# Regrouping the token chunks of a retention-plus-MLP kernel: the first chunk of every sequence first, decay in the mask, weights loaded by turns, a trailing output layer in group 0

## The chip, the cores and the metric

One core of a Trainium2 chip runs the whole program. The metric is the device time in microseconds (us). A profile gives in addition the span from the first to the last instruction of one execution, some 2 us less than its device time. "Granted clock" is the share of TensorE's full clock that the profile records. Engines are named as in the profile: PE is TensorE (matmuls), PEld its weight loads, ACT is ScalarE, DVE is VectorE, POOL is GpSimd. `L217` is line 217 of the kernel that the profile belongs to.

## The reference

```python
# q, k, v: (4 sequences, 8 heads, 768 positions, 64), float32
for t in range(S):                                   # a decaying state, one step per position
    state = gamma * state + k[t] outer v[t]          # gamma per head, 1 - 2**(-5-h)
    y[t]  = q[t] @ state / sqrt(64)
x = y as (3072 tokens, 512)
h = x @ w_in                                         # 512 x 2048
g = h + sin(alpha * h)**2 / (alpha + 1e-9)
out = g @ w_out                                      # 2048 x 512
```

## The kernel before

A sequence is cut into six chunks of 128 positions, 24 chunks in all. Inside a chunk the recurrence becomes two matrix products with a triangular mask. A state carries it from chunk to chunk, so chunk c needs the chunks before it in its sequence. For each chunk the stages are T (transposes of q and k), A (scores times mask, into `aT`) and M (scores times V, the state's part, the update of the state, the scaled result into `xT`).

Finished chunks form groups. For a group of up to four chunks (512 columns) the first layer runs as 16 tiles f = 0..15. Meanwhile the attention of the next group and the output layer of the previous one run in the gaps.

```python
groups = [3, 2, 4, 4, 4, 4, 3]                       # chunks of each group, in the sequences' order

def ff_in(g, f, square):                             # one first-layer tile
    ph = psum.tile([128, n], F32, name="ph", tag="mm", bufs=4)
    for i in range(KS):                              # KS = 4
        nc.tensor.matmul(ph, w_in[...f...], xT[g][:, i, :], ...)          # L217
    nc.scalar.activation(out=s, in_=ph, func=ACTF.Sin, ...)               # L220
    # square of s on ACT (L222) or on DVE (L224)
    return lambda: nc.vector.scalar_tensor_tensor(gT[g][:, f, :], s, rec_alpha[...], ph, ...)   # L225

def ff_out(g, ts, f):                                # one of 16 output steps of one chunk
    if f == 0:
        po[g, ts] = psum.tile([128, d_model], F32, name="po", tag="mm", bufs=4)
    nc.tensor.matmul(po[g, ts], gT[g][:, f, ...], w_out[:, f, :], start=(f == 0), stop=(f == FF - 1))   # L234
```

In PSUM the kernel gives the scores `pa` 128x1024 float32, the attention output `ty` 128x512, the state `ps` 128x256, and the rotating tag `mm` four buffers of 128x512. A bank in this document is one such buffer of 512 float32 columns; `pa` is as large as two. First-layer tiles (`ph`) and output accumulators (`po`) share the four of `mm`. A `ph` bank is free only after the `gT` update, three engine steps later; a `po` bank only after 16 steps.

V is multiplied by a decay (`kg`) before use. GpSimd does this for chunks 9 to 23, and VectorE for the early ones. Loads are issued by GpSimd, in this order: chunks 1 and 2, three quarters of w_in, chunk 3, the last quarter, chunk 4, four quarters of w_out, the other chunks.

Of the kernel before, what the change touches and what calls it, by code (L numbers as in the profile page):

```python
# [15 lines left out]
def kernel(  # L16
# [12 lines left out]

    nc = tc.nc  # L30
# [9 lines left out]
    assert S % C == 0 and D == 64 and H % 2 == 0 and d_model == 512  # L40
    scale = 1.0 / math.sqrt(D)
# [3 lines left out]
    groups = [3, 2, 4, 4, 4, 4, 3]  # L45
    assert sum(groups) == NJ
    NG = len(groups)
    first = [sum(groups[:g]) for g in range(NG)]
    group_of = [g for g, n in enumerate(groups) for _ in range(n)]
# [19 lines left out]
    def load(name, src, j):  # L69
        t = big.tile([128, H, D], BF16, name=f"{name}r", tag=f"{name}r", bufs=NJ)  # L70
        nc.gpsimd.dma_start(out=t, in_=chunk_of(src, j))  # L71
        raw[name, j] = t

    def load_chunk(j):
        for name, src in (("q", q), ("k", k), ("v", v)):
            load(name, src, j)
# [13 lines left out]
    for name, src in (("q", q), ("k", k)):  # L90
        near[name] = big.tile([128, H, D], F32, name=f"{name}0")
        nc.sync.dma_start(out=near[name], in_=chunk_of(src, 0))
        raw[name, 0] = big.tile([128, H, D], BF16, name=f"{name}b")
# [7 lines left out]
    load("v", v, 0)  # L101
# [5 lines left out]
    nc.vector.tensor_scalar(ident, tio, pos[:, 0:1], None, op0=ALU.is_equal)  # L107

# [5 lines left out]
    lg = consts.tile([128, H], F32, name="lg")  # L114
    for h in range(H):
        nc.vector.memset(lg[:, h:h + 1], lng[h])
# [4 lines left out]
    for p in range(NP):  # L121
        nc.scalar.activation(out=qg[:, 0, p, :], in_=tio, func=ACTF.Exp, scale=lgp[:, p:p + 1])
    kg = consts.tile([128, NCH, H], F32, name="kg")
    nc.scalar.activation(out=kg, in_=expo, func=ACTF.Exp, scale=-1.0)
    step = consts.tile([128, NCH, NP], F32, name="step")
    for c in range(1, NCH):
        nc.scalar.activation(out=step[:, c, :], in_=lgp, func=ACTF.Exp, scale=float(C * c))
# [4 lines left out]
    mask01 = consts.tile([128, 128], BF16, name="mask01")  # L132
    nc.vector.tensor_scalar(mask01, tio, pos[:, 0:1], None, op0=ALU.is_ge)
    mask_bc = mask01[:, None, :].to_broadcast([128, H, 128])
# [10 lines left out]
    def scale_v(j, eng):  # L145
        eng.tensor_mul(raw["v", j], raw["v", j], kg[:, j % NCH, :, None].to_broadcast([128, H, D]))  # L146

    def open_T(j, tag="ty", bufs=1):
        st["pt", j] = psum.tile([128, 2 * NP, 128], BF16, name="pt", tag=tag, bufs=bufs)
        st["qkT", j] = work.tile([128, 2 * NP, 128], BF16, name="qkT", tag="qkT", bufs=3)  # L150

    def half_T(j, i):
        for p in range(NP):
            nc.tensor.transpose(st["pt", j][:, i * NP + p, :],  # L154
                                raw["qk"[i], j][:, 2 * p:2 * p + 2, :].rearrange("p h d -> p (h d)"), ident)

    def stage_T(j):
        open_T(j)
        half_T(j, 0)
        half_T(j, 1)  # L160
        nc.scalar.copy(st["qkT", j], st["pt", j])  # L161

    def stage_A(j):
# [8 lines left out]
        nc.vector.tensor_mul(aT.rearrange("p e n t -> p (e n) t"), pa.rearrange("p e n t -> p (e n) t"), mask_bc)  # L172
        st["aT", j] = aT

    def stage_M(j):
        b, c = divmod(j, NCH)
        g = group_of[j]
        if j == first[g]:
            xT[g] = work.tile([128, KS, groups[g] * C], BF16, name="xT", tag="xT", bufs=3)
# [12 lines left out]
        last = c == NCH - 1  # L192
        if not last:
            if c == 0:
                st["ps"] = psum.tile([128, NP, D], F32, name="ps", tag="ps")
            ps = st["ps"]
            for p in range(NP):
                for e in range(2):
                    nc.tensor.matmul(ps[64 * e:64 * e + 64, p, :], raw["k", j][:, 2 * p + e, :], vs[:, 2 * p + e, :],  # L199
                                     start=(c == 0 and p == 0), stop=True, skip_group_check=True)  # L200
        o = (j - first[g]) * C
        nc.vector.tensor_mul(xT[g][:, :, o:o + C], py, qg[:, c])  # L202
        if not last:
            for e in range(2):
                r = slice(64 * e, 64 * e + 64)
                nc.scalar.copy(s_bd[(c + 1) % 2][r, :, r], ps[r, :, :])  # L206
# [4 lines left out]
    def ff_in(g, f, square):  # L211
        n = groups[g] * C
        if f == 0:
            gT[g] = work.tile([128, FF, n], BF16, name="gT", tag="gT", bufs=2)
        ph = psum.tile([128, n], F32, name="ph", tag="mm", bufs=4)
        for i in range(KS):
            nc.tensor.matmul(ph, w_in[:, i, f * 128:(f + 1) * 128], xT[g][:, i, :],  # L217
                             start=(i == 0), stop=(i == KS - 1))
        s = work.tile([128, n], F32, name="s", tag="s", bufs=4)
        nc.scalar.activation(out=s, in_=ph, func=ACTF.Sin, scale=alpha_sb[:, f:f + 1])  # L220
        if square == "A":
            nc.scalar.activation(out=s, in_=s, func=ACTF.Square)  # L222
        else:
            (nc.vector if square == "D" else nc.gpsimd).tensor_mul(s, s, s)  # L224
        return lambda: nc.vector.scalar_tensor_tensor(  # L225
            gT[g][:, f, :], s, rec_alpha[:, f:f + 1], ph, op0=ALU.mult, op1=ALU.add)

    out_view = out.rearrange("(t p) n -> p t n", p=128)
    po = {}

    def ff_out(g, ts, f):
# [4 lines left out]
        if f == FF - 1:  # L236
            o_sb = work.tile([128, d_model], F32, name="o_sb", tag="o_sb", bufs=3)
            if g == NG - 1 and ts == groups[g] - 1:
# [5 lines left out]
            nc.sync.dma_start(out=out_view[:, first[g] + ts, :], in_=o_sb)  # L244

    def out_pieces(g):
        if g == 0:
            todo = [(ts, f) for f in range(FF) for ts in (0, 1)] + [(2, f) for f in range(FF)]
        else:
            todo = [(ts, f) for ts in range(groups[g]) for f in range(FF)]  # L250
        return [lambda ts=ts, f=f: ff_out(g, ts, f) for ts, f in todo]


    LATE = 9
    todo = [lambda j=j: load_chunk(j) for j in (1, 2)]
    todo += [lambda i=i: load_w_in(i) for i in range(3)]
    todo += [lambda: load_chunk(3), lambda: load_w_in(3), lambda: load_chunk(4)]
    todo += [lambda i=i: load_w_out(i) for i in range(WP)]
    todo += [lambda j=j: load_chunk(j) for j in range(5, LATE)]
    for j in range(LATE, NJ):  # L260
        todo += [lambda j=j: load_chunk(j)]
        if j > LATE + 1:
            todo += [lambda j=j: scale_v(j - 2, nc.gpsimd)]
    todo += [lambda j=j: scale_v(j, nc.gpsimd) for j in (NJ - 2, NJ - 1)]
    for fn in todo:
        fn()
# [5 lines left out]
    def idle_work(n, w=512):  # L272
        for _ in range(n):
            nc.tensor.matmul(scratch[:, :w], warm[:, :128], warm[:, :w], start=True, stop=True)  # L274


    idle_work(9)
    nc.vector.tensor_copy(raw["q", 0], near["q"])
    open_T(0, "mm", 4)
    half_T(0, 0)  # L280
    nc.scalar.copy(st["qkT", 0][:, :NP, :], st["pt", 0][:, :NP, :])
    nc.vector.tensor_scalar_mul(qg[:, 0], qg[:, 0], scale)
    decay_table(1)
    idle_work(6)
    nc.vector.tensor_copy(raw["k", 0], near["k"])
    half_T(0, 1)
    nc.scalar.copy(st["qkT", 0][:, NP:, :], st["pt", 0][:, NP:, :])
    scale_v(0, nc.vector)
    idle_work(4)
    stage_A(0)  # L290
    open_T(1, "mm", 4)
    half_T(1, 0)
    half_T(1, 1)
    nc.scalar.copy(st["qkT", 1], st["pt", 1])
    scale_v(1, nc.vector)
    for t in s_bd:
        nc.vector.memset(t, 0.0)
    idle_work(3)
    stage_M(0)
    idle_work(1)  # L300
    stage_A(1)
    open_T(2, "mm", 4)
    half_T(2, 0)
    idle_work(2)
    half_T(2, 1)
    nc.scalar.copy(st["qkT", 2], st["pt", 2])
    scale_v(2, nc.vector)
    nc.tensor.transpose(pal, alpha_row, ident_f)
    idle_work(3)
    stage_M(1)  # L310
    idle_work(1)
    stage_A(2)
    nc.scalar.copy(alpha_sb, pal)
    sin0 = consts.tile([128, 1], F32, name="sin0")
    nc.scalar.activation(out=sin0, in_=warm[:, 0:1], func=ACTF.Sin)
    decay_table(2)
    nc.vector.tensor_scalar_add(rec_alpha, alpha_sb, 1e-9)
    nc.vector.reciprocal(rec_alpha, rec_alpha)
    idle_work(5)
    stage_M(2)  # L320
    idle_work(3)


    def phase(g, outs, att, squares):

        no, done = len(outs), 0
        for f in range(FF):
# [4 lines left out]
            while done < no * (f + 1) // FF:  # L332
                outs[done]()
                done += 1

# [14 lines left out]

    phase(0, [], {2: [G(3)], 5: [G(4)], 9: [T(3), V(3)], 11: [A(3)], 13: [G(5)]}, "AAD")
    outs = out_pieces(0)
    stage_T(4)
    scale_v(4, nc.vector)
    for fn in outs[:4]:
        fn()
    stage_A(4)
    stage_M(3)
    for fn in outs[4:8]:
        fn()  # L360
    stage_M(4)
    phase(1, outs[8:], {7: [T(5), V(5)], 8: [A(5)], 9: [T(6), V(6)], 10: [A(6), M(5)], 11: [T(7), V(7)],
                        12: [A(7), M(6)], 13: [T(8), V(8)], 14: [A(8), M(7)]}, "AAAD")
    stage_M(8)
    for g in range(2, NG):
        att = {}
        if g + 1 < NG:
            js = list(range(first[g + 1], first[g + 1] + groups[g + 1]))
# [40 lines left out]
```

## Time and profile before

| | before |
|---|---|
| device time, median of 3 runs | 235.52 us (234.64 to 238.43) |
| profiled span, mean granted clock | 233.0 us, 0.997 |
| PE busy | 214.8 us, 92% of the span |
| PE's largest wait: first-layer matmul for a gT update | 3.5 us in 5 waits |

The page of the kernel before, its table of 40 time slices (5.8 us each; a digit is the busy share in tenths; PEclk is the granted clock in tenths):

```profile
PE   7998867988889998999999999999999999999992
PEclk9999999999999999999999999999999999999998
```

PE has gaps in the first 16 slices (to about 93 us) and is full afterwards. A change can therefore gain only in the first 93 us, or by taking PE work away.

The same by stage, from the windows view of the kernel before. Columns: stretch, its length, then busy time and count of PE, PEld, DVE, ACT and POOL, granted clock, DMA share, GB/s. The borders are the first Sin of groups 0, 1, 2 and 3:

```profile
0.00:18.40 18.40, 16.43 (x154) 8.67 (x157) 12.91 (x39) 10.27 (x25) 14.65 (x23) 1.00 1.46 159
18.40:39.90 21.50, 16.26 (x152) 9.47 (x151) 17.77 (x30) 16.97 (x34) 10.74 (x14) 1.00 1.69 187
39.90:65.60 25.70, 22.97 (x247) 14.75 (x251) 18.13 (x32) 19.92 (x41) 23.28 (x26) 1.00 2.34 150
65.60:94.40 28.80, 26.75 (x240) 13.96 (x242) 22.34 (x29) 23.92 (x39) 28.80 (x33) 1.00 1.75 125
94.40:233.00 138.60, 132.39 (x955) 66.93 (x969) 75.62 (x104) 96.83 (x160) 6.90 (x7) 1.00 0.18 44
```

Groups 0 and 1 leave PE idle for 5.2 and 2.7 us. The last row is the dense part.

PE's waits in the kernel before (line, what it waited for: us in total, times, longest):

```profile
PE ph L217 <- DVE gT L225: 3.5, 5, 1.3
PE ph L217 <- DVE xT L202: 2.3, 4, 0.8
PE pa L169 <- ACT qkT L161: 2.0, 6, 0.6
```

The timeline of the kernel before at the start of group 1, with two output accumulators open, which leaves two `mm` banks for first-layer tiles (start, duration, engine, line, operation; in brackets, how long the engine was idle before and what released it):

```profile
40.12 0.60 PE L217 MATMUL ph<-xT,w_in 128*128 128x256 bf16 x4
...
40.76 0.47 ACT L220 ACTIVATE s<-ph,alpha_sb 128x256 f32<-128x256 f32 x1
...
41.27 0.42 ACT L222 ACTIVATE s<-s 128x256 f32<-128x256 f32 x1
...
41.72 0.48 DVE L225 SCALAR_TENSOR_TENSOR gT<-s,rec_alpha,ph 128x256 bf16<-128x256 f32 x1 [0.39 <-ACT s L222]
...
42.25 0.60 PE L217 MATMUL ph<-xT,w_in 128*128 128x256 bf16 x4
```

This is one life of a bank: matmuls at 40.12, Sin, square, gT update, and the same bank's next tile at 42.25 us. That is 2.13 us per bank for 256 columns, or one tile in about 1.07 us with two banks.

### The profile page before, as it was taken

The page shows a single profiled execution, that of the slowest core. Times are in us where ns is not written, and L with a number is a line of the kernel's source. Part 1 is how long each engine was busy: PE and PEld are TensorE (multiplying, and loading weights), DVE is VectorE, ACT ScalarE, POOL GpSimd, SP SyncE. Part 2 cuts the span into 40 slices and gives each one's busy share as a digit, 9 for nine tenths or more (in the row PEclk, how much of TensorE's full clock was granted, in tenths as well). Part 3 has the DMA queues.
Part 4 walks back from the last instruction along what each step waited for, and adds up shares of the span by engine and source line. Part 5 has one row for each costly group of instructions (what it writes and reads, how often), then busy time and mean ns, then how long its engine had stood idle before and what let it go on. Part 6 is the DMA issues. An engine that isn't in the chain of part 4 may idle for free.

```text
span 233.0 us, 4372 instructions
## 1 busy us (share of the span) xinstructions
PE 214.8 (92%) x1737; PEld 113.8 (49%) x1766; DVE 146.8 (63%) x233; ACT 167.9 (72%) x297; POOL 84.4 (36%) x99
## 2 busy tenths in 40 slices
PE   7998867988889998999999999999999999999992
PEld 3554435555545454445555454455445545555440
DVE  6695996578846799646656656576557575445400
ACT  5478984787868886787787786786787876777420
POOL 8964734987999999930000000000000000000000
PEclk9999999999999999999999999999999999999998
DMA  9999999999999999970110110110111011111111
GB/s 131 141 197 184 184 207 171 155 150 184 114 153 108 111 147 113 141 88 3 48 45 0 48 45 1 48 45 1 48 45 45 3 45 45 48 45 45 45 71 67
DMA packets 82612, 20.48 MB, mean 88 GB/s; under 512 B 75408, under 2 KB 79520, under 8 KB 82592
## 3 DMA queue, kind: packets, MB, share of 16 engines
q0 software_dynamic: 77024, 13.37, 76.4%
q1 hardware_dynamic: 5568, 6.83, 8.5%
q8 instruction: 14, 0.23, 0.4%
q14 instruction: 6, 0.05, 0.1%
HBM read 27.27 MB, written 6.29 MB: 144 GB/s over the span
## 4 chain that ended last, share of the span: by engine, by line
PE 72%; DVE 16%; ACT 7%; issue 3%; DVEq 0%; ACTq 0%
PE po L234 31%; PE ph L217 27%; DVE aT L172 5%; DVE gT L225 4%; PE scratch L274 4%; ACT s L220 3%; PE pt L154 3%; PE pa L169 3%; DVE xT L202 3%; ACT qkT L161 3%; DVE s L224 2%; PE py L186 2%; PE py L190 2%; ACT s L222 1%; DVE qg L130 1%
## 5 line engine op out<-in xcount | busy, mean ns | idle before, releaser
L225 DVE SCALAR_TENSOR_TENSOR gT<-s,rec_alpha,ph 128x512 bf16<-128x512 f32 (+2 forms) x112 | 74.2, 669 | 52.3 <-ACT s L222 51.2
L217 PE MATMUL ph<-xT,w_in 128*128 128x512 bf16 (+2 forms) x444 | 99.5, 348 | 6.0 <-DVE gT L225 3.5
L234 PE MATMUL po<-w_out,gT 128*128 128x512 bf16 x361 | 95.4, 379 | 2.2 <-issue 1.4
L220 ACT ACTIVATE s<-ph,alpha_sb 128x512 f32<-128x512 f32 (+2 forms) x112 | 69.8, 626 | 36.1 <-PE ph L217 35.0
L217 PEld LDWEIGHTS <-w_in 128*128 128x128 bf16 x448 | 43.6, 98 | 51.6 <-issue 8.7
L234 PEld LDWEIGHTS <-gT 128*128 128x128 bf16 x384 | 34.7, 98 | 33.4 <-issue 0.5
L222 ACT ACTIVATE s<-s 128x512 f32<-128x512 f32 (+2 forms) x82 | 46.6, 568 | 2.6
L172 DVE TENSOR_TENSOR aT<-pa,mask 128x1024 bf16<-128x1024 f32 x24 | 29.3, 1222 | 6.7 <-PE pa L169 6.6
L224 DVE TENSOR_TENSOR s<-s 128x512 f32<-128x512 f32 (+2 forms) x30 | 19.5, 651 | 9.4 <-ACT s L220 9.4
L71 POOL DMA_DIRECT2D vr<-in_v_dram x24 | 21.9, 913 | 3.9 <-DMA w_out<-in_moe_w_out_dram 1.7
L71 POOL DMA_DIRECT2D qr<-in_q_dram x23 | 21.3, 927 | 3.3 <-DMA w_out<-in_moe_w_out_dram 1.7
L71 POOL DMA_DIRECT2D kr<-in_k_dram x23 | 20.4, 889 | 4.7 <-DMA w_out<-in_moe_w_out_dram 3.2
L161 ACT COPY qkT<-pt 128x1024 bf16<-128x1024 bf16 x21 | 21.0, 1000 | 0.7 <-PE pt L154 0.7
L243 ACT COPY o_sb<-po 128x512 f32<-128x512 f32 x23 | 13.5, 590 | 8.1 <-PE po L234 8.1
L206 ACT CAST s_bd<-ps 64x256 bf16<-64x256 f32 x40 | 14.5, 363 | 5.6 <-PE ps L199 4.1
L202 DVE TENSOR_TENSOR xT<-py,qg 128x512 bf16<-128x512 f32 x24 | 16.3, 679 | 2.5 <-PE py L190 2.5
L146 POOL TENSOR_TENSOR vr<-vr,kg 128x512 bf16<-128x512 bf16 x15 | 16.2, 1083 | 3.9 <-ACT s L222 2.1
L274 PE MATMUL scratch<-warm 128*128 128x512 bf16 x35 | 11.5, 462 | 1.4 <-DVE warm L105 1.2
L169 PE MATMUL pa<-qkT 64*128 64x128 bf16 x192 | 9.5, 219 | 2.3 <-ACT qkT L161 2.0
L169 PEld LDWEIGHTS <-qkT 64*128 64x128 bf16 x192 | 5.4, 94 | 11.5 <-ACT qkT L161 5.7
L190 PE MATMUL py<-aT,vr 128*64 128x128 bf16 x192 | 9.5, 220 | 0.5 <-DVE xT L202 0.4
L154 PE MATMUL pt<-ident,qr 128*128 128x128 bf16 x92 | 8.9, 219 | 1.0 <-DVE xT L202 1.0
(53 smaller groups left out, 89.2 us busy)
## 6 DMA issues: line engine op xcount, KB each, us to landing
out_dram<-o_sb SPq DMA_DIRECT2D x24, 256.0 KB, 2.0
vr<-in_v_dram POOLq DMA_DIRECT2D x24, 128.0 KB, 5.3
qr<-in_q_dram POOLq DMA_DIRECT2D x23, 128.0 KB, 4.9
kr<-in_k_dram POOLq DMA_DIRECT2D x23, 128.0 KB, 5.1
w_in<-in_moe_w_in_dram POOLq DMA_DIRECT2D x4, 512.0 KB, 10.2
w_out<-in_moe_w_out_dram POOLq DMA_DIRECT2D x4, 512.0 KB, 12.1
q<-in_q_dram SPq DMA_DIRECT2D x1, 256.0 KB, 3.3
k<-in_k_dram SPq DMA_DIRECT2D x1, 256.0 KB, 4.1
```

What stands on the lines that cost most here:

```text
L71: nc.gpsimd.dma_start(out=t, in_=chunk_of(src, j))
L161: nc.scalar.copy(st["qkT", j], st["pt", j])
L169: nc.tensor.matmul(pa[:, e, p, :], qkT[r, NP + p, :], qkT[r, p, :], start=(p == 0), stop=True, skip_group_check=True)
L172: nc.vector.tensor_mul(aT.rearrange("p e n t -> p (e n) t"), pa.rearrange("p e n t -> p (e n) t"), mask_bc)
L202: nc.vector.tensor_mul(xT[g][:, :, o:o + C], py, qg[:, c])
L217: nc.tensor.matmul(ph, w_in[:, i, f * 128:(f + 1) * 128], xT[g][:, i, :], start=(i == 0), stop=(i == KS - 1))
L220: nc.scalar.activation(out=s, in_=ph, func=ACTF.Sin, scale=alpha_sb[:, f:f + 1])
L222: nc.scalar.activation(out=s, in_=s, func=ACTF.Square)
L224: (nc.vector if square == "D" else nc.gpsimd).tensor_mul(s, s, s)
L225: return lambda: nc.vector.scalar_tensor_tensor(gT[g][:, f, :], s, rec_alpha[:, f:f + 1], ph, op0=ALU.mult, op1=ALU.add)
L234: nc.tensor.matmul(po[g, ts], gT[g][:, f, ts * C:(ts + 1) * C], w_out[:, f, :], start=(f == 0), stop=(f == FF - 1))
L274: nc.tensor.matmul(scratch[:, :w], warm[:, :128], warm[:, :w], start=True, stop=True)
```

## The change

The intent has three parts.

1. The first chunk of each of the four sequences needs no state. These four become group 0, so the opening loses its serial state chain. The decay and the scale go into the mask of a first chunk (`dec`), so V needs no scaling there.
2. Quarters of w_in and w_out are loaded by turns, so that the output layer of group 0 can begin early.
3. Group 0's output layer trails its own first layer by two tiles: step f-2 of two output chunks runs after tile f. Group 1 then has less output work left. Groups 1 and 2 trail one chunk each in the same way.

```diff
-    groups = [3, 2, 4, 4, 4, 4, 3]
+    order = [b * NCH for b in range(B)]
+    order += [b * NCH + c for b in range(B) for c in range(1, NCH)]
+    sizes = [4, 2, 4, 4, 4, 4, 2]
...
+    for j in order[1:3]:
+        load_chunk(j)
+    load_w_in(0)
+    load_chunk(order[3])
+    load_w_out(0)
+    for i in range(1, WP):
+        load_w_in(i)
+        load_w_out(i)
+    for j in order[4:LATE]:
+        load_chunk(j)
...
+    for h in range(H):       # scale * gamma**(t-s), then times the triangular mask
+        nc.scalar.activation(out=dec[:, h % 2, h // 2, :], in_=tio, func=ACTF.Exp, scale=lng[h], bias=back[:, h:h + 1])
...
+        m = dec.rearrange("p e n t -> p (e n) t") if j % NCH == 0 else mask_bc
...
-    def phase(g, outs, att, squares):
+    def phase(g, outs, own, att, squares, slots=range(FF), lag=2):
...
+            if f >= lag:
+                for ts in own:
+                    ff_out(g, ts, f - lag)
...
+    for f in range(4):                          # chunks e0, e1, e2; the fourth comes late
+        add = ff_in(0, f, "A" if f % 2 == 0 else "D", (0, n3))
+        if f == 1:
+            stage_T(e3)
+        add()
+    stage_A(e3)
+    idle_work(2)
+    for f in (0, 1):
+        for ts in (0, 1):
+            ff_out(0, ts, f)                    # two accumulators open from here
+    stage_M(e3)
+    for f in range(4):                          # the fourth chunk's part of tiles 0 to 3
+        ff_in(0, f, "A", (n3, 4 * C))()
...
+    phase(0, [], (0, 1), {7: [G(2)], 9: [G(3)], 11: [G(4)], 13: [G(5)]}, "AAD", range(6, FF))
...
+    stage_T(P[4]); scale_v(P[4], nc.vector); fill(5); stage_A(P[4]) ...   # dense fill, then group 1
+    for j in order[1:B]:
+        scale_v(j, nc.gpsimd)                   # three V scalings in a row on GpSimd
...
+    left = {2: (out_pieces(1, (1,)), (0,)), 3: (out_pieces(2, (1, 2, 3)), ())}
```

`idle_work(n)` issues n matmuls whose results are not used; they only keep PE active. The changed opening has fewer of them.

## The prediction

> **What bounds it now.** TensorE (PE) bounds the core from about 95 us on: by the table of windows PE is busy 33.2 of 34.1 us (95.5 to 129.6 us). In the timeline four 512-column matmuls take 0.86 us [...], one chunk's attention 1.46 us. All PE work is then about 200 us, and the last matmul ends at 228.8 us: some 28 us are idle or filler, all early. By stage: 13 us before the first first-layer matmul (17.45 us), 7 us until 39.3 us, 4 us in group 1 (to 64.5 us), 4 us in group 2 (to 95.5 us), where ScalarE and VectorE limit (25.0 and 22.5 of 31 us busy). Only saved early PE idleness shortens the run.
>
> **What the change removes and moves.** Group 0 loses the serial state (copies 0.36 us each), V scaling (0.68 us) and the qg multiply; I expect the first first-layer matmul at 15.8 us, limited about equally by the chain and by w_in's first quarter (landed near 15.4 us before). But its three chunks hold 1.4 us less PE work, so little idleness is saved. Eight Exp of 0.32 us and a 1.2 us table-times-mask enter the opening chain. Weight pieces take 2.55 us each by the landings; by turns, w_in's last lands near 33 us instead of 25.6 us, w_out's last stays near 36 us.
>
> **What it adds.** The fourth chunk joins late: its attention should end near 24 us (its mask multiply queues behind gT updates), the 128-column repeats near 27 us. From then two trailing accumulators hold two of the four "mm" PSUM buffers, so first-layer tiles alternate between two. One cycle by the trace: matmul to Sin 1.07, Sin 0.62, square 0.66, gT 0.75 us, with gaps 3.15 us; over two buffers 1.6 us per tile. Check: group 1 before, also with two accumulators, 256 columns, reuses a buffer every 2.13 us, as its chain says. Twelve tiles last until about 48 us, later than loads require (39 us). At equal PE work, before was at about 45 us. The dense fill that follows wins two back. Group 1 then has 18 us of PE work against 22 us of ScalarE, and loses 4 to 5 us; group 2, again with two accumulators, takes 31 to 33 us for 26.6 us of PE work. From group 4 nothing changes; the tail (two chunks, not three) is the same PE work in another order.
>
> **Prediction.** My sum gives 2 to 6 us longer, but so hand-tuned an order may hide waits that I counted, so I lean back: 237.0 us, 8 in 10 between 230.5 and 243.0. Faster by over 2%: 0.20; within 2%: 0.50; slower by over 2%: 0.30.
>
> **What would show it.** First first-layer matmul near 15.8 us; PE's wait list headed by first-layer matmuls waiting for gT updates in group 0 (1.6 us per tile from 27 to 48 us), not for DMA; group 1's first tile at 57 us, group 2's at 80 us; PE busy over 95% from group 4; last matmul to end of span unchanged, 4.2 us.
>
> **What would make it wrong.** If the two-buffer cycle is shorter, or the fourth chunk joins by 20 us, group 0 ends at the load limit, near 40 us, and the change gains about 5 us. If w_in's later quarters land after 33 us, or the sparser filler leaves PE longer at the 0.43 us per filler matmul that it shows at the start, it loses more.

Four matmuls in 0.86 us can be read from the timeline of the kernel before (98.77 to 99.63 us).

## The result

| | before | after |
|---|---|---|
| device time, median of 4 runs each | 235.32 us | 252.68 us (249.80 to 255.67) |
| ratio after/before, fast runs | | 1.0716 (95%: 1.0619 to 1.0814): slower |
| profiled span, granted clock | 233.0 us, 0.997 | 251.3 us, 0.970 |
| PE busy | 214.8 us | 219.4 us |

A ratio here and below is the mean time of one kernel's fast runs over that of the other's fast runs of the same rounds, so it is not quite the ratio of the quoted medians. One of the four runs after was slow and left out of the ratio. Outputs were correct in every run.

The page after, the same rows of its table of slices (6.3 us each):

```profile
PE   6797498478878788789999999999999999999993
PEclk9689779999999999999999999999999999999998
```

PE is fuller from slice 19 on than anywhere earlier, as before, but that stage begins later. The clock row has dips in the second and third slices and in the fifth and sixth.

The windows view after, between the first Sins of the groups:

```profile
0.00:19.60 19.60, 15.22 (x104) 7.35 (x106) 10.62 (x36) 10.96 (x29) 15.47 (x24) 0.83 1.55 167
19.60:67.20 47.60, 35.32 (x249) 17.15 (x252) 31.16 (x42) 25.95 (x47) 36.58 (x41) 0.93 1.96 168
67.20:92.20 25.00, 19.54 (x244) 13.14 (x246) 18.14 (x32) 18.77 (x40) 25.00 (x28) 1.00 1.72 112
92.20:123.90 31.70, 27.87 (x249) 14.16 (x251) 21.50 (x29) 23.99 (x40) 8.34 (x9) 1.00 0.46 44
123.90:251.30 127.40, 121.41 (x908) 63.34 (x922) 71.43 (x102) 92.33 (x160) 0.00 (x0) 0.99 0.11 40
```

This gives the ledger on which all that follows rests. From the first Sin of group 3 the kernel after needs 127.4 us, and before 138.6, because ten chunks are behind it by then instead of nine. It would tie if group 3 began at 233.0 - 127.4 = 105.6 us. It begins at 123.9 us. **The loss of the profiled run, 18.3 us, lies wholly ahead of group 3, in the opening and groups 0 to 2.** Group 1 finds PE busy for 19.54 of 25.0 us: it has less PE work than before (22.97) and takes nearly as long.

PE's waits after:

```profile
PE ph L249 <- DVE gT L256: 14.6, 19, 3.7
PE py L227 <- DVE aT L193: 2.1, 1, 2.1
...
PE pal L298 <- DMA alpha_row<-in_moe_alpha_dram: 1.6, 1, 1.6
...
PE pt L174 <- DVE kb L294: 1.3, 1, 1.3
```

No wait for weights stands here. First-layer matmuls wait for gT updates 14.6 us instead of 3.5, and one such wait lasted 3.7 us.

The timeline after in group 0, one life of a first-layer bank at 512 columns:

```profile
38.49 1.03 PE L249 MATMUL ph<-xT,w_in 128*128 128x512 bf16 x4
...
39.56 0.69 ACT L251 ACTIVATE s<-ph,alpha_sb 128x512 f32<-128x512 f32 x1
...
40.31 0.68 DVE L255 TENSOR_TENSOR s<-s 128x512 f32<-128x512 f32 x1
...
41.03 0.75 DVE L256 SCALAR_TENSOR_TENSOR gT<-s,rec_alpha,ph 128x512 bf16<-128x512 f32 x1
...
41.83 1.02 PE L249 MATMUL ph<-xT,w_in 128*128 128x512 bf16 x4
```

The bank is used at 38.49 and again at 41.83 us. Tiles begin at 37.20, 38.49, 40.44, 41.83, 43.69 and 45.07 us, two banks taking turns: 1.6 us per tile, as predicted. The PE work of such a step, four first-layer and two output matmuls, is 1.3 us (six times 0.215, a quarter of the 0.86 us that four such matmuls take in the kernel before).

Two things were not predicted. The first is the clock, in the windows view after:

```profile
4.20:7.60 3.40, 1.17 (x11) 0.57 (x9) 2.47 (x4) 2.61 (x8) 3.40 (x5) 0.99 1.79 169
7.60:14.40 6.80, 6.19 (x46) 3.36 (x47) 3.18 (x5) 3.25 (x13) 5.58 (x7) 0.50 1.99 174
...
24.70:28.10 3.40, 1.02 (x16) 0.83 (x16) 1.32 (x2) 1.07 (x3) 1.52 (x2) 0.99 1.25 208
28.10:34.90 6.80, 5.58 (x19) 2.42 (x19) 3.34 (x7) 3.31 (x9) 1.97 (x3) 0.50 1.43 196
```

PE was busy 1.17 of 3.4 us, and for the next 6.8 us the granted clock is 0.50. The same happened at 24.7 us, where the fourth chunk joined (1.02 of 3.4 us, then 0.50 for 6.8 us). In the kernel before PE was busy for all 3.40 us of the stretch from 4.2 to 7.6 us, and the clock stayed at 1.00. Both half-rate stretches here are 6.8 us long. Not every sparse stretch is followed by one: from 45.1 us PE is busy 1.43 of 3.4 us, and the clock stays at 1.00 in the 3.4 us after it.

The second is in the timeline after, from 45.4 us:

```profile
45.46 3.55 POOL L107 TENSOR_TENSOR vr<-vr,kg 128x512 bf16<-128x512 bf16 x3
45.47 2.65 DVE L255 TENSOR_TENSOR s<-s 128x512 f32<-128x512 f32 x1 [0.45 <-ACT s L251]
...
48.03 1.52 DVE L154 TENSOR_TENSOR qg<-qg,step 128x512 f32<-128x512 f32 x1
...
49.48 1.39 DVE L256 SCALAR_TENSOR_TENSOR gT<-s,rec_alpha,ph 128x512 bf16<-128x512 f32 x2
...
50.27 1.02 PE L249 MATMUL ph<-xT,w_in 128*128 128x512 bf16 x4 [3.74 <-DVE gT L256]
```

While GpSimd scales three V tiles, VectorE's square takes 2.65 us instead of 0.68, and the table 1.52 instead of 0.68. The gT updates come late, and PE waits 3.74 us. The square is stretched 3.9 times. "The collision" below means this: a VectorE operation beside GpSimd's V scalings that takes longer than is usual for its kind. By what mechanism it comes about, the traces do not show.

### The profile page after: what moved, and what is told of

It reads as the page before. It is cut to its first block, busy times and chain, and to the rows that moved or that the text cites. A ratio compares the mean times of both kernels' runs of the same rounds, so it can differ in the third digit from the quotient of the medians.

```text
span 251.3 us, 4417 instructions
## 1 busy us (share of the span) xinstructions
PE 219.4 (87%) x1742; PEld 115.1 (46%) x1773; DVE 152.8 (61%) x240; ACT 172.0 (68%) x314; POOL 85.4 (34%) x100
## 4 chain that ended last, share of the span: by engine, by line
PE 62%; DVE 15%; ACT 14%; issue 4%; DMA 2%; SPq 1%; ACTq 0%; DVEq 0%
PE ph L249 26%; PE po L266 25%; ACT s L251 7%; DVE gT L256 6%; DVE s L255 3%; ACT qkT L180 3%; DVE aT L193 3%; ACT s L253 3%; PE pa L189 3%; PE pt L174 2%; DMA alpha_row<-in_moe_alpha_dram 2%; PE py L223 2%; PE py L227 2%; DVE xT L234 2%; PE scratch L288 2%
## 5 line engine op out<-in xcount | busy, mean ns | idle before, releaser
L249 PE MATMUL ph<-xT,w_in 128*128 128x512 bf16 (+3 forms) x457 | 103.0, 347 | 16.2 <-DVE gT L256 14.6
L256 DVE SCALAR_TENSOR_TENSOR gT<-s,rec_alpha,ph 128x512 bf16<-128x512 f32 (+3 forms) x116 | 75.5, 654 | 62.6 <-ACT s L253 61.1
L251 ACT ACTIVATE s<-ph,alpha_sb 128x512 f32<-128x512 f32 (+3 forms) x116 | 71.1, 613 | 48.1 <-PE ph L249 46.2
L266 PE MATMUL po<-w_out,gT 128*128 128x512 bf16 x362 | 98.1, 381 | 3.2 <-issue 1.4
L249 PEld LDWEIGHTS <-w_in 128*128 128x128 bf16 x464 | 45.3, 99 | 64.8 <-issue 24.7
L266 PEld LDWEIGHTS <-gT 128*128 128x128 bf16 x384 | 34.9, 98 | 34.7 <-DVE gT L256 2.2
L253 ACT ACTIVATE s<-s 128x512 f32<-128x512 f32 (+3 forms) x84 | 46.5, 553 | 2.7
L255 DVE TENSOR_TENSOR s<-s 128x512 f32<-128x512 f32 (+2 forms) x32 | 21.6, 676 | 11.9 <-ACT s L251 11.7
L193 DVE TENSOR_TENSOR aT<-pa,mask 128x1024 bf16<-128x1024 f32 x20 | 24.4, 1221 | 4.6 <-PE pa L189 4.6
L76 POOL DMA_DIRECT2D kr<-in_k_dram x23 | 20.7, 898 | 5.5 <-DMA w_out<-in_moe_w_out_dram 3.4
L107 POOL TENSOR_TENSOR vr<-vr,kg 128x512 bf16<-128x512 bf16 x17 | 18.8, 1115 | 1.7 <-DMA vr<-in_v_dram 1.7
L210 ACT CAST s_bd<-ps 64x256 bf16<-64x256 f32 x40 | 14.4, 360 | 4.0 <-PE ps L203 3.5
L234 DVE TENSOR_TENSOR xT<-py,qg 128x512 bf16<-128x512 f32 x20 | 13.7, 683 | 2.2 <-PE py L227 2.2
L288 PE MATMUL scratch<-warm 128*128 128x512 bf16 x26 | 9.5, 503 | 1.4 <-DVE warm L122 1.2
```

Source lines behind the costliest of these rows:

```text
L76: nc.gpsimd.dma_start(out=t, in_=chunk_of(src, j))
L107: eng.tensor_mul(raw["v", j], raw["v", j], kg[:, j % NCH, :, None].to_broadcast([128, H, D]))
L193: nc.vector.tensor_mul(aT.rearrange("p e n t -> p (e n) t"), pa.rearrange("p e n t -> p (e n) t"), m)
L234: nc.vector.tensor_mul(x, py, qg[:, c])
L249: nc.tensor.matmul(ph, w_in[:, i, f * 128:(f + 1) * 128], xT[g][:, i, lo:hi], start=(i == 0), stop=(i == KS - 1))
L251: nc.scalar.activation(out=s, in_=ph, func=ACTF.Sin, scale=alpha_sb[:, f:f + 1])
```

## The experiments

The theory after the first look: the trailing output layer costs most, because two open accumulators leave two banks (1); the half clock (2) and the collision (3) add to it. Rivals: the load order (4), the late join of the fourth chunk (5), and a floor of group 1 that makes all shortening of its PE work worthless (6). Sixteen kernels ran. Those under one lettered heading were run on the same chip, with its own runs of the kernel before; the five headings used five chips, so a difference between kernels of two headings also holds what the chips differ by (the kernel before took 234.96 to 235.50 us on them, by the medians). "Group 3 at" is the first Sin of group 3 in the profile.

### A. Take out one suspect each

**trail_off** takes the trailing output out of group 0; all 64 of its output steps come after it.

```diff
-    for f in (0, 1):
-        for ts in (0, 1):
-            ff_out(0, ts, f)
...
-    phase(0, [], (0, 1), {7: [G(2)], ...}, "AAD", range(6, FF))
+    phase(0, [], (), {7: [G(2)], ...}, "AAD", range(6, FF))
-    outs = out_pieces(0, (2, 3))
+    outs = out_pieces(0, (0, 1, 2, 3))
```

> The changed kernel with group 0's output layer not trailing: no accumulator is open in group 0, all 64 of its output matmul steps come after it. Theory 'buffers' (two trailing accumulators leave two PSUM banks for first-layer tiles): the tile period of f=4 to 15 falls from about 1.9 us (26.2 us for 12 tiles, the stall of 3.7 us included) to about 1.2 us, group 0 ends some 6 to 9 us earlier, 32 matmuls (6.9 us) move to the fill and group 1, where half of them fit into idle time; ratio to the kernel before 1.04 to 1.06 instead of 1.07. Theory 'clock and GpSimd alone' (buffers do not matter): the period stays near 1.6 us outside the stall, and the moved matmuls make the run longer, ratio 1.08 or more.

Measured: 242.24 us, ratio 1.0305 (1.0242 to 1.0369), span 240.7 us. Group 0 took 33.2 us instead of 47.6, and group 1 28.8 instead of 25.0. Group 3 began at 113.3 instead of 123.9 us. The windows view of trail_off over group 0 (for after it is the second row above, 47.60 us):

```profile
19.50:52.70 33.20, 27.25 (x224) 14.26 (x223) 26.75 (x42) 23.92 (x46) 22.09 (x24) 0.95 1.82 166
```

The part of the change meant to fill PE's gaps costs 10.6 us of the 18.3. The 6.9 us of PE work that it moved (32 output matmuls of 0.215 us) shortened group 1 by only 3.8 us.

**v_late** moves the three GpSimd V scalings behind five chunk loads.

```diff
-    for j in order[1:B]:
-        scale_v(j, nc.gpsimd)
     for n, j in enumerate(order[LATE:]):
         load_chunk(j)
+        if n == 4:
+            for i in order[1:B]:
+                scale_v(i, nc.gpsimd)
```

> The changed kernel with the three GpSimd scalings of the first chunks' V moved behind five more chunk loads, so that they run at about 60 us and not at 45 us in group 0. Theory 'GpSimd collision': VectorE's square of 2.65 us and the first-layer wait of 3.7 us at 45 to 50 us vanish, group 0 ends about 3 to 3.5 us earlier, ratio about 1.057. Rival (VectorE was late for another reason): the wait stays where it is and the ratio stays at 1.07.

Measured: 253.2 us, ratio 1.0774 (1.0714 to 1.0834): no gain. Group 1 did begin 3.7 us earlier (63.5 instead of 67.2 us), but groups 1 and 2 took 27.6 and 32.4 us instead of 25.0 and 31.7. The collision had only moved. The timeline of this kernel, at its new place:

```profile
62.61 4.12 DVE L107 TENSOR_TENSOR vr<-vr,kg 128x512 bf16<-128x512 bf16 x1
...
63.11 4.52 POOL L107 TENSOR_TENSOR vr<-vr,kg 128x512 bf16<-128x512 bf16 x4
```

A VectorE scaling of 0.68 us took 4.12 us, 6.1 times as long, beside four GpSimd ones. This makes the collision surer and says nothing of its worth.

**warm** puts more filler matmuls into the two sparse stretches and the alpha transpose behind the first scores, so that PE no longer waits for alpha's load.

```diff
-    stage_T(e0, True)
-    nc.tensor.transpose(pal, alpha_row, ident_f)
-    idle_work(2)
+    stage_T(e0, True, 6)          # six fillers between the q and the k transposes
+    idle_work(5)
     stage_A(e0)
+    nc.tensor.transpose(pal, alpha_row, ident_f)
...
+    zero_work(8)                  # and 3, and 2 per repeat, around the late join
```

> The changed kernel with more filler matmuls where TensorE idled: six between the transposes of q and k of the first chunk, five instead of two before its attention, the alpha transpose moved behind it, and matmuls that add zero to an open accumulator around the fourth chunk. Theory 'clock': the granted clock stays 1.00 in both stretches that were at half (7.6 to 14.4 us and 28.0 to 34.9 us), the first first-layer matmul moves from 18.7 to about 17 us, group 0 ends 3 to 4 us earlier, ratio about 1.055. Rival (the half clock only fell on time that was idle anyway): clock 1.00 but the end moves by less than 1 us, ratio 1.07.

Measured: 250.35 us, ratio 1.0623 (1.0543 to 1.0704), granted clock of the profiled run 1.000, span 246.5. Its window over the stretch that had been sparse (columns as above):

```profile
4.20:7.60 3.40, 3.40 (x21) 1.75 (x20) 2.39 (x3) 2.61 (x8) 3.40 (x5) 1.00 1.85 170
```

The filler cures the clock: over the next 6.8 us (7.6 to 14.4) it was 1.00, where after has 0.50. In the second place PE was busy 3.22 of 3.4 us (24.7 to 28.1), and from 28.1 to 34.9 us the clock was 1.00 again. So it is shown for these two places that the sparse stretch brought the half rate. The first first-layer matmul began at 16.45 us instead of 18.67, and group 1 7.3 us earlier. Of this, 4.8 us remained in the profiled span, since group 1 then took 27.5 us instead of 25.0. The intervals of this ratio and of the change's overlap, so the gain in time is small and not sharply measured.

**win_first** loads the last three quarters of w_in ahead of the last three of w_out (the first quarter of w_out stays second).

```diff
     load_w_out(0)
     for i in range(1, WP):
         load_w_in(i)
+    for i in range(1, WP):
         load_w_out(i)
```

> The changed kernel with the weight pieces not by turns: the last three quarters of w_in before the last three of w_out. Theory 'buffers': loads do not limit group 0 (its tiles come later than the pieces land), so nothing moves by more than 1 us, ratio 1.07. Rival 'loads': w_in's last quarter lands about 5 us earlier and group 0 ends 3 to 5 us earlier, ratio about 1.05.

Measured: 256.47 us in the median, but three of four runs were slow (the fast one took 250.44), so there is no ratio. In the profile, from a slow run, Sin of tile 4 came no earlier (33.3 against 32.4 us), but 10.2 us from 26.4 us on were at half clock there, so this alone shows little. That group 0 of after does not wait for w_in rests on its own wait list, in which no wait of PE for w_in stands.

### B. Keep the trailing output, mend its costs; then the first part of the change alone

**banks_pa** keeps the trailing output but puts both accumulators into the two `pa` banks, idle during most of group 0. First-layer tiles get four banks.

```diff
-        if f == 0:
+        if f == 0 and g == 0 and ts < 2:
+            if ts == 0:
+                st["po2"] = psum.tile([128, 2, d_model], F32, name="po2", tag="pa")
+            po[g, ts] = st["po2"][:, ts, :]
+        elif f == 0:
```

> The changed kernel, trailing output layer kept, but its two accumulators put into the two PSUM banks of the attention scores, which are idle in group 0, so that first-layer tiles have four banks; same matmuls, the first four output steps a little later. Theory 'buffers': the tile period of f=4 to 15 falls from 1.6 us (outside the stalls) to 1.3 to 1.4 us, now set by TensorE's own 1.3 us per tile, group 0 ends 4 to 6 us earlier, ratio 1.05 to 1.06. Rival (the trailing matmuls themselves, in order between the tiles, slow group 0, as trail_off cannot tell): period stays near 1.6 us and the ratio at 1.07.

Measured: 247.34 us, ratio 1.0516 (1.0464 to 1.0569), span 246.9. From Sin of tile 4 to Sin of tile 15 it took 14.7 us (32.0 to 46.7) where after took 22.2 (32.4 to 54.6). The windows view over these stretches, first of after, then of banks_pa:

```profile
32.40:54.60 22.20, 16.44 (x66) 6.70 (x66) 15.59 (x19) 11.88 (x19) 19.61 (x22) 0.94 2.33 141
```

```profile
32.00:46.70 14.70, 14.49 (x69) 6.37 (x66) 12.05 (x19) 11.69 (x19) 10.95 (x13) 1.00 2.29 161
```

With four banks tiles follow each other every 1.3 us (PE busy 14.49 of 14.7 us) and not every 1.6: the banks set the pace of the tiles. Not all of the 7.5 us is theirs: after has the wait of 3.74 us and 2.5 us at half clock in its stretch, while in banks_pa the three GpSimd scalings began at 46.2 us, when these tiles were nearly done. Group 0 fell from 47.6 to 39.9 us, but the profiled span by only 4.4: group 2 now took 34.3 us instead of 31.7. There a square of VectorE beside GpSimd took 2.15 us (0.69 is usual), PE waited 2.73 us, and 3.4 us at half clock followed (from 99.7 us).

**v_dve** does those three V scalings on VectorE, between the tiles of group 0.

```diff
-    phase(0, [], (0, 1), {7: [G(2)], 9: [G(3)], ...
+    phase(0, [], (0, 1), {6: [V(P[1])], 7: [G(2)], 8: [V(P[2])], 9: [G(3)], 10: [V(P[3])], ...
-    for j in order[1:B]:
-        scale_v(j, nc.gpsimd)
```

> The changed kernel with the three V scalings on VectorE inside group 0 (0.68 us each at f=6, 8, 10) in place of GpSimd. v_late only moved the collision (a scaling of VectorE then took 4.12 us at 62.6 us beside four scalings of GpSimd). Theory 'collision': without any place where three GpSimd scalings run back to back, both stalls vanish, group 1 starts about 3 us earlier and keeps it, the run ends 2.5 to 3.5 us earlier, ratio about 1.06. Rival (the time is lost in group 1 to something else whenever group 1 starts earlier, as v_late and warm also suggest): group 1 starts earlier, but group 2 does not by more than 1 us, ratio 1.07.

Measured: 252.69 us, ratio 1.0744 (1.0678 to 1.0810). Group 1 began 2.6 us earlier, and took 27.0 instead of 25.0 us. The collision is real and costs group 0 time. What it costs the end v_dve cannot tell, because it takes away only these three GpSimd scalings: those of later chunks still run in groups 1 and 2. There one square took 1.35 us (0.43 is usual for 256 columns, at 77.7 us) and one 2.49 us (0.69 is usual, at 96.3 us), and 3.4 us of group 1 were at half clock (from 82.2 us). Over the whole trace VectorE's stretched operations, each against the median of its kind, are too long by 4.4 us in after and 4.1 us in v_dve. Only p1_vdve (heading C) takes all of them away.

**fixed** combines banks_pa, v_dve and the filler of warm: the three costs mended in group 0 with the trailing output kept (in groups 1 and 2 two accumulators stay open and GpSimd still scales V). **part1** keeps only the first part of the change: no trailing output in group 0, the load order of win_first, filler, the three V scalings of v_dve on VectorE.

> banks_pa, v_dve and warm together: the whole change kept, the three costs taken away. If they are all that is wrong: first first-layer matmul at 16.5 us, group 0 ends near 46 to 47 us, group 1 starts near 56 us and takes 24 us, ratio 1.01 to 1.02. If there is a fourth cost of a similar size the ratio stays above 1.03.

> Only the first part of the change (first chunks of all sequences as first group, decay in the mask), with w_in whole before most of w_out, no trailing output layer in group 0, V scaled by VectorE and the filler of warm. Group 0 is then limited by ScalarE (about 1.2 us per tile), ends near 43 us, group 1 starts near 50 us and has 18 + 6.9 us of TensorE work; ratio 0.99 to 1.02. If the new grouping itself costs, above 1.02.

Measured: fixed 246.90 us, ratio 1.0504 (1.0433 to 1.0574); part1 241.04 us, ratio 1.0255 (1.0204 to 1.0305). So even a trailing output that has full clock, four banks and no collision in group 0 costs 5.9 us against none. (The two differ in the load order too; in neither does PE wait for a weight in group 0.) The windows view over group 1, first of part1, then of fixed:

```profile
53.10:80.30 27.20, 25.82 (x279) 16.24 (x277) 19.42 (x32) 19.95 (x42) 26.60 (x29) 1.00 1.94 145
```

```profile
59.00:85.80 26.80, 19.84 (x249) 13.15 (x247) 20.70 (x32) 18.91 (x41) 26.80 (x30) 1.00 1.77 121
```

Here is the deeper reason. Group 1 has 25.82 us of PE work in part1 and 19.84 in fixed, and takes 27.2 and 26.8 us. Moving 6 us of PE work out of it gives 0.4. The same work lengthened the stretch from group 0 to group 1: 40.5 us in fixed, 35.0 in part1. So far rival 6 holds. In part1 PE itself is nearly full in group 1 (25.82 of 27.2 us). In fixed it is not, and neither is ScalarE (18.9 of 26.8 us) or VectorE (20.7); GpSimd is busy nearly throughout in both (26.60 and 26.80 us), mostly with issuing loads (in fixed its seven V scalings of 1.08 us are 7.6 us of it). What limits fixed is a chain of waits. Its timeline in group 1, where PE's longest wait ends:

```profile
66.21 1.66 DVE L257 TENSOR_TENSOR s<-s 128x256 f32<-128x256 f32 x1
...
67.79 1.21 DVE L195 TENSOR_TENSOR aT<-pa,mask 128x1024 bf16<-128x1024 f32 x1
...
68.92 0.68 DVE L236 TENSOR_TENSOR xT<-py,qg 128x512 bf16<-128x512 f32 x1
...
69.52 0.86 DVE L258 SCALAR_TENSOR_TENSOR gT<-s,rec_alpha,ph 128x256 bf16<-128x256 f32 x2
...
70.04 0.60 PE L251 MATMUL ph<-xT,w_in 128*128 128x256 bf16 x4 [2.17 <-DVE gT L258]
```

Two gT updates, for which the two banks of first-layer tiles wait, stand on VectorE behind a mask multiply and an xT of the next group's chunks, and behind a square stretched from 0.43 to 1.66 us beside GpSimd. The critical view of this group (59 to 86 us) puts at least 52% of the chain on VectorE. So two open accumulators and the collision are part of the floor in fixed. How short group 1 would be without them, and with less PE work, was not tried.

### C. Why the first part alone was still slower

Three edits to part1, one at a time, then together. **p1_oneacc**: the chunk that trails in groups 1 and 2 opens its accumulator only when the previous group's output is done, so that one is open at a time. **p1_join**: the fourth chunk joins at tile 8, with no stop for it, and w_out's first quarter is loaded behind w_in. **p1_all** has all three edits. **p1_vdve**: all V scaling on VectorE.

```diff
# p1_oneacc
-            if f >= lag:
-                for ts in own:
-                    ff_out(g, ts, f - lag)
-            while done < no * (n + 1) // n0:
-                outs[done]()
+            while done < (no + len(mine)) * (n + 1) // n0:
+                if done < no:
+                    outs[done]()
+                elif mine[done - no][1] <= f - lag:
+                    ff_out(g, *mine[done - no])
+                else:
+                    break
# p1_join
-    for f in range(4): ... (0, n3) ...; stage_A(e3); idle_work(14); stage_M(e3) ...
+    att = {1: [lambda: stage_T(e3)], 4: [lambda: stage_A(e3)], 6: [lambda: stage_M(e3)], ...}
+        add = ff_in(0, f, "AAD"[f % 3], (0, n3) if f < 8 else (0, 4 * C))
# p1_vdve
-            scale_v(order[LATE + n - 2], nc.gpsimd)
-                att.setdefault(max(a - 1, 0), []).append(T(j))
+                att.setdefault(max(a - 1, 0), []).extend([T(j), V(j)])
```

> part1, but in groups 1 and 2 the trailing accumulator opens only after the previous group's last one has closed, so one is open at a time and first-layer tiles have three banks, with the same matmuls in each group. Theory 'buffers': group 2 (first Sin to first Sin of the next group) falls from 31.6 us to about 29 us, what the kernel before takes (28.8 us), ratio from 1.026 to about 1.015. Rival (group 2 is limited by ScalarE and VectorE work alone): no change within 0.5 us.

> part1, but the fourth chunk joins without stopping the others: eight tiles of 384 columns run on while its attention is done between them, then eight of 512, then eight of 128 columns; w_in is loaded whole before w_out. Theory 'late join' (ScalarE idles about 7 us while group 0 waits for the fourth chunk: 11.3 us for the first four tiles where 4.4 us would do): group 0 shortens from 35.0 us by 3 to 5 us although four more small tiles add 2.5 us, ratio about 1.01. Rival (group 0 is limited by the loads): it shortens by less than 1 us.

> part1 with every scaling of V on VectorE (0.68 us each), none on GpSimd. Theory 'collision': the stretched VectorE instructions (1.9 us too long in all in part1's trace) are gone and groups 1 and 2 shorten by 1 to 2 us, ratio about 1.02. Rival (VectorE's added 2.7 us per group costs as much): ratio unchanged at 1.026 or up.

> p1_oneacc, p1_join and p1_vdve together. If the three add up: 239.4 us of span less 3, 4 and 1 to 2 us, ratio 0.99 to 1.00. If they share one cause or give back later, above 1.01.

| | median us | ratio (95%) | group 3 at |
|---|---|---|---|
| part1 (heading B) | 241.04 | 1.0255 (1.0204 to 1.0305) | 112.0 |
| p1_oneacc | 238.00 | 1.0102 (1.0040 to 1.0164) | 108.5 |
| p1_join | 241.03 | 1.0243 (1.0195 to 1.0291) | 112.0 |
| p1_vdve | 240.33 | 1.0213 (1.0164 to 1.0261) | 110.8 |
| p1_all | 236.16 | 1.0039 (0.9991 to 1.0087) | 106.9 |

One open accumulator gives nearly all that the single edits give (3.5 us at group 3, of which 0.5 come back behind it, in the 127.9 instead of 127.4 us from there to the end). The windows view over group 2, first of part1, then of p1_oneacc:

```profile
80.30:112.00 31.70, 28.28 (x253) 14.15 (x250) 21.77 (x29) 24.01 (x40) 17.93 (x20) 1.00 0.99 77
```

```profile
79.60:108.50 28.90, 27.09 (x250) 14.34 (x252) 23.23 (x28) 23.91 (x40) 19.29 (x21) 1.00 1.14 88
```

Group 2 takes 28.9 instead of 31.7 us, which is what it took in the kernel before (28.8). The edit for the late join (rival 5) gave nothing by itself. It is no clean test of the join: it also takes the filler away, adds four repeats of 128 columns, and packs nine tables and V scalings behind tiles 8 to 15. Its profile has 3.4 us at half clock in group 0 (from 41.4 us), and the mean clock is 0.983 to 0.993 in its runs against 0.996 to 1.000 in part1's. p1_vdve's ratio lies inside the interval of part1, so it shows no clear gain of its own, though no stretched VectorE operation is left in its trace (1.9 us too long in part1's). In part1, then, the collision is not worth anything that can be measured.

With all three the first part ties with the kernel before. Its windows view between groups 0 and 1:

```profile
42.00:52.90 10.90, 10.50 (x117) 5.94 (x118) 7.03 (x12) 5.78 (x14) 10.21 (x13) 0.85 3.16 149
```

For 10.9 us ScalarE is busy only 5.78. This is the dense fill of output matmuls, in which the fifth and sixth chunk get their attention because their loads stand behind all the weights. PE is busy, but the chain of Sin, square and gT update stands still. Two more things stand ahead of it in p1_all: VectorE is busy for all of 28.1 to 38.4 us, with those tables and scalings, and the clock is at half from 38.4 to 45.2 us.

### D. Those two chunks loaded between the quarters of w_in

**early** loads the fifth and sixth chunk between the quarters of w_in and gives them their attention inside group 0; w_out moves back. Group 1's own chunks no longer trail, and five of the tables and V scalings leave group 0. It is built on p1_all. **before_vdve** is the kernel before with all V scaling on VectorE, to see whether that alone would help it.

```diff
# early, against p1_all
-    for i in range(1, WP):
-        load_w_in(i)
+    load_w_in(1)
+    load_chunk(order[4])
+    load_w_in(2)
+    load_chunk(order[5])
+    load_w_in(3)
...
+    att = {1: [T(e3)], 4: [A(e3)], 6: [M(e3)], 7: [G(1)], 8: [V(P[0])], 9: [T(P[4]), V(P[4])], 10: [SK(P[0])],
+           11: [A(P[4])], 13: [M(P[4])], 14: [T(P[5]), V(P[5])], 15: [G(2)]}
...
+                    att[a + 1].extend([V(j - 1), SK(j - 1)])
```

> p1_all, but the second and third chunk of the first sequence are loaded between the quarters of w_in, ahead of w_out, and their attention is done inside group 0 (as the kernel before does with its fourth and fifth chunk), not in a fill of 9 us after it; the scalings and decay tables that are not needed yet move to groups 1 and 2, and group 1's own trailing output to group 2. Theory 'fill' (what is left of the loss is ScalarE's idle time between group 0 and group 1, which the load order by turns forces, as it puts those chunks behind all weights): group 1's first Sin moves from 52.9 to about 47 us, group 3's from 106.9 to about 103 us, ratio about 0.985. Rival (ScalarE and VectorE are full anyway and the work only moves): group 3's first Sin stays within 1.5 us of 106.9 us, ratio 1.00.

> The kernel before with all scalings of V from the tenth chunk on done by VectorE (0.68 us each) in place of GpSimd. Theory 'collision is a cost wherever it occurs': before's trace shows one stretched VectorE instruction (1.75 us where 0.69 is usual), so it gains at most 1 us, ratio 0.995 to 1.00, and the collision is no part of what before does better. Rival: a gain or loss of 1% or more.

Measured: early 237.00 us, ratio 1.0093 (1.0002 to 1.0183); before_vdve 234.48 us, ratio 0.9976 (0.9953 to 0.9999). The second is within a quarter per cent: the kernel before loses almost nothing to the collision (the stretched operation that I found in it is one square of 1.75 us, at 90.94 us). In early the wanted effect was there: from group 0 to group 1 it took 26.6 us instead of 35.6, and group 3 began at 102.6 us. But group 4 then took 38.1 us. PE's waits in early:

```profile
PE ps L208 <- DVE vr L107: 3.9, 2, 1.9
```

This was a slip of mine: the V scaling of a first chunk stood directly ahead of the state update that reads it, and PE waited 1.9 us for it twice. After the first of these waits 3.4 us at half clock follow (from 150.1 us).

### E. The slip mended, and one step further

**early2** puts that scaling two tiles earlier. **early3** is early2 with the fourth chunk joining at tile 6 (counted from 0) instead of 8, with fewer repeats.

```diff
# early2, against early
-                    att[a + 1].extend([V(j - 1), SK(j - 1)])
+                    att[a + 1].append(SK(j - 1))
+                    att[max(a - 1, 0)].append(V(j - 1))
# early3, against early2
-    att = {1: [T(e3)], 4: [A(e3)], 6: [M(e3)], ...
+    att = {1: [T(e3)], 3: [A(e3)], 5: [M(e3)], ...
-        add = ff_in(0, f, "AAD"[f % 3], (0, n3) if f < 8 else (0, 4 * C))
+        add = ff_in(0, f, "AAD"[f % 3], (0, n3) if f < 6 else (0, 4 * C))
```

> early with one slip of mine mended: the scaling of a first chunk's V stood directly ahead of the matmuls that need it, and TensorE waited for it twice 1.9 us in group 4, which took 38.1 us instead of 34.3. The scaling now stands two tiles earlier. Theory 'fill' (early did gain some 4 us up to group 3 and gave them back there): group 4 takes 34.3 us again, the span falls from 236.2 to about 232.4 us, ratio 0.99 to 1.00. Rival: the wait only moves, group 4 stays above 36 us.

> early2 with the fourth chunk joining at the seventh tile, not the ninth: two small tiles less (0.66 us of ScalarE each against 0.28 us of a wide tile's share), so group 0 should take 0.7 us less if ScalarE limits it there (26.3 of 28 us busy in early). Ratio 0.985 to 0.995.

Measured: early2 232.30 us (231.79 to 233.07, six runs), ratio 0.9890 (0.9864 to 0.9916), span 230.7, granted clock 1.000. early3 234.04 us, ratio 0.9955 (0.9920 to 0.9990): a miss. Its group 0 began 1.0 us later (18.9 against 17.9 us) and took 27.6 us against 27.0. The edit does not touch what comes before group 0, so the first of these is no effect of it. In four of early3's six runs the mean clock is 0.989 or 0.990, in all of early2's 0.993 or more; the profiled run is none of the four, so where the clock fell is not known. The windows view of early2 over the opening, most of group 0, and the stretch into group 1 and through it:

```profile
0.00:18.00 18.00, 15.07 (x114) 7.21 (x116) 10.77 (x38) 10.69 (x29) 15.34 (x24) 1.00 1.59 164
18.00:44.50 26.50, 20.24 (x206) 11.69 (x208) 22.43 (x38) 24.79 (x52) 13.46 (x17) 1.00 1.72 186
44.50:71.50 27.00, 26.47 (x283) 17.10 (x285) 21.63 (x40) 20.51 (x45) 25.34 (x30) 1.00 2.39 170
```

ScalarE is busy 24.79 of 26.5 us in group 0, and PE 26.47 of 27.0 in group 1. early2 beats both kernels. It keeps the first chunks first and the decay in the mask. It has no trailing output in group 0, at most one accumulator open in groups 1 and 2, V scaling on VectorE, more filler in the opening, and loads the fifth and sixth chunk between the quarters of w_in. Its interval lies wholly below 1. PE now waits 2.0 us for w_in, so the loads have become a limit for the first time.

### The ledger of all profiled runs that carry the argument

First Sin of group 0, time from there to the first Sin of groups 1, 2 and 3, and the span, worked out from the timelines with the borders rounded to 0.1 us. Each row is one profiled run:

| kernel | group 0 at | group 0 | group 1 | group 2 | group 3 at | span |
|---|---|---|---|---|---|---|
| before | 18.4 | 21.5 (3 chunks) | 25.7 | 28.8 | 94.4 (9 chunks behind it) | 233.0 |
| after | 19.6 | 47.6 | 25.0 | 31.7 | 123.9 | 251.3 |
| trail_off | 19.5 | 33.2 | 28.8 | 31.8 | 113.3 | 240.7 |
| warm | 17.4 | 42.5 | 27.6 | 31.6 | 119.1 | 246.5 |
| banks_pa | 20.0 | 39.9 | 25.3 | 34.3 | 119.5 | 246.9 |
| v_dve | 20.0 | 44.6 | 27.0 | 32.7 | 124.3 | 251.7 |
| fixed | 18.5 | 40.5 | 26.8 | 33.2 | 119.0 | 246.4 |
| part1 | 18.1 | 35.0 | 27.2 | 31.7 | 112.0 | 239.4 |
| p1_oneacc | 17.8 | 35.0 | 26.8 | 28.9 | 108.5 | 236.3 |
| p1_all | 17.3 | 35.6 | 25.8 | 28.2 | 106.9 | 234.7 |
| early2 | 17.9 | 27.0 | 27.0 | 30.9 | 102.8 | 230.7 |

From "group 3 at" to the end all regrouped kernels here need 127.4 to 127.9 us; what they differ in lies before. A tie stands at 105.6.

## Why the prediction was wrong

I predicted 237.0 us (230.5 to 243.0) with "within 2%" as the likeliest outcome. The run took 252.68 us and was slower by 7%. It had the direction of its own sum and the mechanism, two banks by turns, right. The step that failed is the sum of the time until group 2, and above all its term "Twelve tiles last until about 48 us": these tiles lasted until 56.7 us. Group 2's first tile came 11.2 us later than forecast, of which 8.7 us are this term, 0.9 the fill and 1.6 group 1. The lean back, for which no number stood, added to the miss. Point by point:

- **What bounds it, and where time can be gained: right.** PE is full from group 3 on in both kernels, the PE work from there is what the regrouping leaves (127.4 us), and the whole difference is early. The tail also stayed: the last matmul ended at 247.2 us, and the span 4.1 later, as predicted (4.2).
- **The two-bank cycle, "1.6 us per tile": right,** with its sign and its size. PE's wait list is headed by first-layer matmuls waiting for gT updates, not for DMA, as predicted. banks_pa shows the cause: with four banks a tile took 1.3 us.
- **"The first first-layer matmul at 15.8 us": wrong,** it came at 18.67. I had counted the chain's operations, but not the clock. The opening keeps PE busy 1.17 of 3.4 us, and the clock was 0.50 for the next 6.8. Added to it are 1.6 us of waiting for alpha's load and 1.3 for the cast of k. The prediction named the sparser filler as a danger and gave it no time. warm brought the matmul to 16.45 us.
- **"Twelve tiles last until about 48 us": mis-sized.** The last gT update ended at 56.7 us. The first 512-column tile began at 30.49 instead of 27 us (3.5 us late, mostly from the opening). The first three tiles took 6.7 us instead of 4.8, under the half clock. The step from 45.07 to 50.27 us lasted 5.2 us instead of 1.6, in the collision of GpSimd and VectorE, which I had not seen in the diff. These add up to 9.0 us; the end of group 0's tiles was 8.7 us late.
- **"Group 1's first tile at 57 us, group 2's at 80 us": wrong,** 66.6 and 91.2. The fill lasted 9.9 us against 9 in my sum, and group 1 24.6 against 23. I had let group 1 follow ScalarE's busy time (22 us). It follows a chain: ScalarE was busy only 18.8 of 25.0 us. With the clock, the banks and the collision mended in group 0, fixed still took 246.9 us. There group 1 began at 59.0 us where the prediction had 57, and took 26.8 us where it had 23; group 2 took 33.2 us where it had 31 to 33.
- **"The dense fill that follows wins two back": wrong in kind.** The fill keeps PE busy, while ScalarE idles (5.78 us of work in 10.9 us in p1_all). early2, in which all but four steps of the fill are gone, went from p1_all's 1.0039 to 0.9890; that VectorE's work in group 0 was lightened and the half clock went is in this too, and was not told apart.
- **Group 2, "31 to 33 us": right** (31.7), and so was the reason, two accumulators: with one, p1_oneacc took 28.9.
- **"I lean back": wrong.** My own sum said 2 to 6 us longer, and no number stood behind moving it down. The sum without the lean would still have missed, by 11 to 15 us.

What the change hoped for failed for one reason above all: it filled PE's gaps with work that group 1 could hold at a smaller cost (3.8 us in trail_off, 0.4 in part1). Take the trailing output out (trail_off) and 10.6 of the 18.3 us come back. Of the rest, 1.3 us come from the filler, three V scalings on VectorE and the load order together (part1), 3.5 from one open accumulator instead of two (p1_oneacc), and 1.6 from the join and the remaining V scaling (p1_all). These sum to 17.0; the last 4.1 us of early2 come from the load order of two chunks with what was moved along with it (heading D), and turn the loss into a gain. The steps were taken in this order and on several chips, one profiled run each, so the size of each holds for its place and roughly. Group 1 is limited by PE in part1 and early2 (25.82 of 27.2 and 26.47 of 27.0 us busy), and by the chain through VectorE in fixed. What stays open is how short it would be with less PE work, one accumulator and no GpSimd scaling beside it.

## What to carry to other kernels

An idle engine was worth filling only as far as the stage that gave the work away got shorter for it (here 0.4 us for 6 us of PE work, fixed against part1): look at what ends last there before moving work out of it. An accumulator that stays open takes a bank from every tile that rotates beside it. Here the cost could be worked out beforehand as one life of a bank divided by the banks that are left: 3.15 us by the prediction, over two banks 1.6 us per tile, and 1.6 measured in after, against 1.3 with four banks in banks_pa, where PE was full. When a diff thins out the opening or adds GpSimd arithmetic beside VectorE arithmetic, check the granted clock and the mean durations first: both changed times that were taken from the trace before (a clock of 0.50 for 6.8 us after a sparse opening, a square of 2.65 us instead of 0.68).
